# Two weight conversions dealt out in steps over the last attention blocks, and the first v's split queued behind the centroid copies

## The chip, the cores and the metric

The kernel runs on one core of a Trainium2 chip. The metric is device time in microseconds (us), the median over runs; less is better. TensorE is PE, its weight load PEld, VectorE DVE, ScalarE ACT, GpSimd POOL; SyncE (SP) issues every DMA of this kernel.

## The reference, cut to what matters

Three parts follow each other: clustered attention, a product of two projections (moe), and a gated one (moe2).

```python
mask = q_assign[:, :, :, None] == k_assign[:, :, None, :]   # argmax over 16 centroids per head
scores = scale * q @ k.T; scores = where(mask, scores, -1e9)
x = softmax(scores) @ v                                     # 2 x 8 heads, 768 tokens, head size 64
x = x.transpose(0, 2, 1, 3).reshape(1536, 512)
h = ((x @ w1) * (x @ w2)) @ w3                              # 512 -> 1024 -> 1024
y = h @ w_out                                               # 1024 -> 512
out = (sigmoid(y @ w_gate) * (y @ w_val)) @ w_out2          # 512 -> 1536 -> 512
```

The weights reach the chip as 64-bit floats (two 32-bit words each) and are converted there. Every operand of a large product is split into a high and a low part (`hi`, `lo`), and a product is three matmuls (L65 to L67).

## The kernel before, in words

**Attention.** The 16 heads make 8 pairs (`pr`), each pair has two heads (`e`), each head three blocks of 256 queries: 48 blocks (`NB`), block number = 6 pr + 3 e + q0/256. The main loop runs `i` from -2 to 48. In one turn it issues the scores 2i+3 and 2i+4 (two 128-query halves of blocks i+1 and i+2: matmuls L315 to L318, then the maximum `nm` on DVE, L319, and the exponential `e` on ACT, L321), the transposes of block i (PE L332, `ph` on ACT L56, `pl` on DVE L59), and the weighted sum with v of block i-1 (L355, L356). So a block has two `nm`, and the scores of turn i = 33 end with the first half of block 35.

**Preparation of a pair** runs beside the blocks of the pair before it: loads of q and k (`load_qk`, L192) and v; splits into hi and lo (`prep_split`: q's on ACT and DVE, k's on POOL for pairs above 0); similarities with the centroids (`prep_sims`, PE L252); the cluster by argmax and its one-hot code (L254 to L277); and DMAs inside SBUF that build the operands QH, KH, QX, KX (`move`, L62).

**The start.** Before pair 0 the centroids are normalised, transposed by PE (L164) and split into `chi` and `clo` on DVE (L168, L169). Eight small POOL copies put them into `cw` (L175), which `prep_sims` needs as weights. `prep_v(0)` splits v on POOL (two L54, two L59). PE runs `warm` transposes (L134) whose result nobody reads: 12, 8, and 70 after the first similarities.

**Conversion of weights** (`f64_split`): a DMA brings a 128x512 tile of 64-bit words (L98, pool tag f64 with 3 buffers), ACT takes the absolute value of the upper words (L102), DVE does five operations in a row (L108 clamp, L110 shift, L111 merge, L112 mask, L113 product; "steps" here), `f_engine` adds (L114), ACT rounds to hi (L115), POOL subtracts for lo (L116). `load_pair` does this twice, for w1 and w2 of one group. The first two pairs of w1 and w2 are converted within attention, at i = NB-12 = 36 and i = NB-6 = 42, each as a whole, with L114 on POOL:

```python
if i in (NB - 12, NB - 6):
    with tc.issue_after(last["DVE"].ins), tc.issue_after(last["ACT"].ins):
        wt.append(load_pair(w12, len(wt), "w12_", nc.gpsimd))
```

`tc.issue_after(x)` puts every instruction of the block that runs on x's engine behind x in that engine's queue. It is a lower bound on the place only. Otherwise each engine's order is set by a list scheduler from the order of the text, its own estimate of when operands are ready, and buffers; an instruction that is ready by that estimate can go ahead of earlier text. Within a queue the order is then fixed, and a waiting instruction holds up all behind it.

**After attention** (L400 on) everything is a long run of matmuls `p` (L65 to L67): first `g_unit`, which needs the two converted pairs, then the other products.

Of the kernel before, what the change touches and what calls it, by code (L numbers as in the profile page):

```python
# [9 lines left out]
F32R = mybir.dt.float32r  # L10
U32 = mybir.dt.uint32
# [5 lines left out]
NP = H // 2  # L17
# [10 lines left out]
def tile_cluster_attention__then__moe__then__gated_moe(  # L28
# [15 lines left out]
    nc = tc.nc  # L44
# [6 lines left out]
    def split(x, hi, lo, hi_engine, lo_engine):  # L51

        if hi_engine is nc.gpsimd:
            nc.gpsimd.tensor_scalar(out=hi, in0=x, scalar1=1.0, scalar2=1.0, op0=ALU.mult, op1=ALU.mult)  # L54
        elif hi_engine is nc.scalar:
            nc.scalar.copy(hi, x)  # L56
        else:
            nc.vector.tensor_copy(hi, x)
        lo_engine.tensor_tensor(out=lo, in0=x, in1=hi, op=ALU.subtract)  # L59
# [20 lines left out]
    ws = ctx.enter_context(tc.tile_pool(name="ws", bufs=2, side="right"))  # L80
# [3 lines left out]
    def f64_split(src, hi, lo, name, f_engine, lo_engine):  # L84

        n = src.shape[-1]
        raw = ws.tile([128, n, 2], U32, tag="f64", name=f"{name}_f64", bufs=3)
        nc.sync.dma_start(raw.rearrange("p n t -> p (n t)"), src.bitcast(U32))  # L98
        low, high = raw[:, :, 0], raw[:, :, 1]
        a = ws.tile([128, n], U32, tag="f64a", name=f"{name}_a", bufs=3)  # L100
        af = a.bitcast(F32)
        nc.scalar.activation(af, high.bitcast(F32), AF.Abs)  # L102
        if cvp:
            nc.gpsimd.tensor_scalar(out=af, in0=af, scalar1=F64_MAX, scalar2=F64_MIN, op0=ALU.min, op1=ALU.max)
            t = cvp["pool"].tile([128, n], U32, tag="t", name=f"{name}_t", bufs=2)
            tf = t.bitcast(F32)
        else:
            nc.vector.tensor_scalar(out=af, in0=af, scalar1=F64_MAX, scalar2=F64_MIN, op0=ALU.min, op1=ALU.max)  # L108
            t, tf = a, af
        nc.vector.tensor_scalar(out=t, in0=a, scalar1=3, scalar2=0x3FFFFFF8, op0=ALU.logical_shift_left, op1=ALU.bitwise_and)  # L110
        nc.vector.scalar_tensor_tensor(out=high, in0=high, scalar=0xC0000000, in1=t, op0=ALU.bitwise_and, op1=ALU.bitwise_or)  # L111
        nc.vector.tensor_scalar(out=t, in0=high, scalar1=0xFF800000, scalar2=None, op0=ALU.bitwise_and)  # L112
        nc.vector.scalar_tensor_tensor(out=tf, in0=low, scalar=2.0 ** -52, in1=tf, op0=ALU.mult, op1=ALU.mult)  # L113
        f_engine.tensor_tensor(out=af, in0=high.bitcast(F32), in1=tf, op=ALU.add)  # L114
        nc.scalar.copy(hi, af)  # L115
        lo_engine.tensor_tensor(out=lo, in0=af, in1=hi, op=ALU.subtract)  # L116

    def load_pair(src, m, what, f_engine=None):
        hl = ws.tile([128, 2, 2, NP, 128], F32R, tag="hl", name=f"{what}{m}")
        for w in range(2):  # L120
            f64_split(src[m, w], hl[:, 0, w].rearrange("p k c -> p (k c)"), hl[:, 1, w].rearrange("p k c -> p (k c)"),
                      f"{what}{m}_{w}", f_engine or nc.vector, nc.gpsimd)
        return hl

    att, cst = ExitStack(), ExitStack()
# [44 lines left out]
    for e in range(2):  # L170
        rows = slice(64 * e, 64 * e + 64)
        for w in range(2):
            base = 64 * w + 32 * e
            for g, src in ((0, chi), (1, clo)):
                nc.gpsimd.tensor_copy(  # L175
                    cw[rows, :, w, base + 16 * g : base + 16 * g + 16],
                    src[rows].bitcast(F32).rearrange("p (n e c) -> p n e c", n=NP, e=2)[:, :, e, :],
                )
# [5 lines left out]
    core = att.enter_context(tc.tile_pool(name="core", bufs=2))  # L184


    raw = {}

    def load_qk(pr):
        for w in range(2):  # L190
            t = core.tile([128, S], F32, tag="raw", name=f"raw{pr}_{w}", bufs=2)
            nc.sync.dma_start(t, qkT[pr, :, w, :])  # L192
            raw[pr, w] = t

    def load_v(pr):
        t = core.tile([128, 2, KT, D], F32, tag="vraw", name=f"vraw{pr}", bufs=1)
        nc.sync.dma_start(t, v[pr])
        raw[pr, "v"] = t


    load_qk(0)


# [24 lines left out]
    def prep_scatter(pr, e):  # L228
        qh, ql, kh, kl = opnd[pr, "hl"]
        r = slice(64 * e, 64 * e + 64)  # L230
        QH = core.tile([96, S], F32R, tag="QH", name=f"QH{pr}_{e}", bufs=3)
        KH = core.tile([96, S], F32R, tag="KH", name=f"KH{pr}_{e}", bufs=3)
        QX = core.tile([128, S], F32R, tag="QX", name=f"QX{pr}_{e}", bufs=3)
        KX = core.tile([128, S], F32R, tag="KX", name=f"KX{pr}_{e}", bufs=3)
        move(QH[0:64], qh[r])
        move(KH[0:64], kh[r])
        move(QX[0:64], qh[r])
        move(QX[64:128], ql[r])
        move(KX[0:64], kl[r])
        move(KX[64:128], kh[r])  # L240
        opnd[pr, e] = (QH, KH, QX, KX)
# [17 lines left out]
    def prep_argmax(pr):  # L259
        sm = opnd.pop((pr, "sm"))  # L260
        mx = core.tile([128, S // 32], F32, tag="mx", name=f"mx{pr}", bufs=2)
        shape = [128, S // 32, C]
        nc.vector.tensor_reduce(out=mx, in_=sm, axis=AX.X, op=ALU.max)
        nc.vector.tensor_tensor(out=sm, in0=sm, in1=mx.unsqueeze(2).broadcast_to(shape), op=ALU.is_ge)
        lead(pr).tensor_tensor(out=sm, in0=sm, in1=dec.unsqueeze(1).broadcast_to(shape), op=ALU.mult)
        opnd[pr, "code"] = sm
# [13 lines left out]
    def prep_mask(pr, e):  # L280
        ohT = opnd[pr, "oh"]
        QH, KH, _, _ = opnd[pr, e]
        if pr == 0:
            nc.scalar.copy(QH[64:96], ohT[32 * e : 32 * e + 32])
            nc.vector.tensor_scalar(out=KH[64:96], in0=ohT[64 + 32 * e : 96 + 32 * e], scalar1=-1.0, scalar2=BIG, op0=ALU.add, op1=ALU.mult)
            return
        move(QH[64:96], ohT[32 * e : 32 * e + 32])
        move(KH[64:96], ohT[64 + 32 * e : 96 + 32 * e])

    def prep_v(pr):  # L290
        vr = raw.pop((pr, "v"))
        for e in range(2):
            vx = core.tile([128, KT, 2, D], F32R, tag="vx", name=f"vx{pr}_{e}", bufs=3)
            split(vr[:, e], vx[:, :, e, :], vx[:, :, 1 - e, :], nc.gpsimd, nc.gpsimd)
            opnd[pr, e, "v"] = vx
# [1 line left out]

    blocks = [(pr, e, q0) for pr in range(NPR) for e in range(2) for q0 in range(0, S, 256)]
    NB = len(blocks)
    exps, pts, avs, acc_x, last = {}, {}, {}, {}, {}  # L300

    def scores(j):

# [84 lines left out]
    def finish_x(pr):  # L388
        b, hp = divmod(pr, NP)
        xa, r = acc_x.pop((pr, "xa")), acc_x.pop((pr, "r"))  # L390
        nc.gpsimd.tensor_tensor(out=xa, in0=xa, in1=r, op=ALU.mult)
        split(xa, x_hl[:, hp, 0, S * b : S * b + S], x_hl[:, hp, 1, S * b : S * b + S], nc.gpsimd, nc.gpsimd)
# [10 lines left out]
    prep_onehot(0)  # L403
    for e in range(2):
        prep_mask(0, e)
    prep_v(0)
    load_qk(1)
    prep_split(1)
    prep_scatter(1, 0)
    wt = []  # L410
    for i in range(-2, NB + 1):
        pr, at = divmod(i, 6)
        nxt = pr + 1 if 0 <= i and pr + 1 < NPR else None
        later = nxt + 1 if nxt and nxt + 1 < NPR else None
        scores(2 * i + 3)
        if nxt and at == 1:
            prep_scatter(nxt, 1)
            prep_argmax(nxt)
        transposes(i, 0)
        if nxt and at == 0:  # L420
            prep_sims(nxt)
        scores(2 * i + 4)
        if nxt and at == 2:
            prep_onehot(nxt)
            for e in range(2):
                prep_mask(nxt, e)
        transposes(i, 1)
        transposes(i, 2)
        if later and at == 2:
            load_qk(later)  # L430
        if later and at == 3:
            load_v(later)
        if i == 0:
            load_v(1)
        weighted_v(i - 1, 0)
        if nxt and at == 2:
            prep_v(nxt)
        weighted_v(i - 1, 1)
        if 0 < pr and i < NB and at == 2:
            finish_x(pr - 1)  # L440
        weighted_v(i - 1, 2)
        if later and at == 3:
            prep_split(later)
            prep_scatter(later, 0)
        if 0 <= i < NB and at == 5:
            sums(pr)
        if i in (NB - 12, NB - 6):
            with tc.issue_after(last["DVE"].ins), tc.issue_after(last["ACT"].ins):
                wt.append(load_pair(w12, len(wt), "w12_", nc.gpsimd))
    finish_x(NPR - 1)  # L450
    att.close()

# [81 lines left out]
    for u, tok in enumerate(units):  # L534
        for c in range(NP):
            p = ps.tile([128, 512], F32, tag="p", name=f"p3_{c}_{u}")
# [14 lines left out]
    for g in range(MG // GS):  # L551
        us = []
        wo2 = p5.tile([128, GS, 2, DM], F32R, tag="wo2", name=f"wo2_{g}", bufs=2)
        for j in range(GS):
            m = g * GS + j
# [11 lines left out]
        for t in range(T // 128):  # L567
            p = ps.tile([128, DM], F32, tag="p", name=f"p5_{g}_{t}")
# [67 lines left out]
```

## Time and profile before

| | |
|---|---|
| median of 3 runs | 816.96 us (816.45 to 820.29) |
| profiled execution | 818.45 us, its span 816.6 us |
| mean granted clock of TensorE in the span | 0.985 of full |
| busy share of the span | PE 95%, DVE 71%, ACT 44%, POOL 42% |
| DMA | 78.05 MB, mean 96 GB/s |
| last `nm` of attention begins | 270.07 us |
| first matmul `p` of the products begins | 277.25 us |

A timeline row gives the start in us, the time in us, engine, line, operation, what is written and read, the tile, how many instructions were merged into the row, and in brackets the idle time of the engine before it with what ended it. A time with "x2" is that of both, from the start of the first to the end of the last.

### The profile page before, as it was taken

The page shows a single profiled execution, that of the slowest core. Times are in us where ns is not written, and L with a number is a line of the kernel's source. Part 1 is how long each engine was busy: PE and PEld are TensorE (multiplying, and loading weights), DVE is VectorE, ACT ScalarE, POOL GpSimd, SP SyncE. Part 2 cuts the span into 40 slices and gives each one's busy share as a digit, 9 for nine tenths or more (in the row PEclk, how much of TensorE's full clock was granted, in tenths as well). Part 3 has the DMA queues.
Part 4 walks back from the last instruction along what each step waited for, and adds up shares of the span by engine and source line. Part 5 has one row for each costly group of instructions (what it writes and reads, how often), then busy time and mean ns, then how long its engine had stood idle before and what let it go on. Part 6 is the DMA issues. An engine that isn't in the chain of part 4 may idle for free.

```text
span 816.6 us, 11246 instructions
## 1 busy us (share of the span) xinstructions
PE 777.5 (95%) x4051; PEld 662.7 (81%) x4051; DVE 580.5 (71%) x856; ACT 360.8 (44%) x711; POOL 342.4 (42%) x356
## 2 busy tenths in 40 slices
PE   6899999999696999999999999999999999999998
PEld 6788888988595888887888888888888888888886
DVE  3898989989978769999999443377761777827222
ACT  1788889889586633344433222223231322012100
POOL 3347657757646354545443111234420444124100
PEclk8999999999888999999999999999999999999999
DMA  8745646556512033444442200022220122200012
GB/s 220 212 132 136 169 124 172 144 132 165 137 42 72 21 130 106 151 130 142 142 155 78 77 1 1 26 77 79 78 80 24 52 77 96 86 1 0 1 65 90
DMA packets 26967, 78.05 MB, mean 96 GB/s; under 512 B 4416, under 2 KB 4512, under 8 KB 26912
## 3 DMA queue, kind: packets, MB, share of 16 engines
q1 hardware_dynamic: 26912, 77.33, 32.2%
q8 instruction: 32, 0.52, 0.3%
q14 instruction: 23, 0.19, 0.1%
HBM read 52.49 MB, written 3.19 MB: 68 GB/s over the span
## 4 chain that ended last, share of the span: by engine, by line
PE 67%; DVE 12%; POOL 8%; ACT 5%; DMA 4%; issue 4%; SPq 0%; DVEq 0%; POOLq 0%; ACTq 0%
PE p L66 17%; PE p L67 17%; PE p L65 17%; PE pt L332 3%; DVE nm L319 2%; DMA raw<-in_qkT_dram 2%; ACT e L321 2%; PE s L315 1%; DVE pl L59 1%; PE sims L252 1%; PE av L356 1%; PE w34p L67 1%; PE av L355 1%; PE w34p L65 1%; PE w34p L66 1%
## 5 line engine op out<-in xcount | busy, mean ns | idle before, releaser
L65 PE MATMUL p<-x,wgv 128*128 128x512 f32 x288 | 112.0, 389 | 0.0
L66 PE MATMUL p<-x,wgv 128*128 128x512 f32 x288 | 112.0, 389 | 0.0
L67 PE MATMUL p<-x,wgv 128*128 128x512 f32 x288 | 112.0, 389 | 0.0
L319 DVE TENSOR_REDUCE nm<-s 128x1 f32<-128x768 f32 x96 | 90.9, 948 | 10.4 <-PE s L318 9.8
L332 PE MATMUL pt<-ident,e 128*128 128x128 f32 x576 | 83.6, 279 | 10.4 <-DVE pl L59 9.5
L59 DVE TENSOR_TENSOR pl<-pt,ph 128x512 fp32r<-128x512 f32 x128 | 85.3, 682 | 7.7 <-ACT ph L56 6.8
L321 ACT ACTIVATE e<-s,nm 128x768 f32<-128x768 f32 x96 | 87.4, 910 | 3.7 <-DVE nm L319 2.8
L332 PEld LDWEIGHTS pt<-ident,e 128*128 128x128 f32 x576 | 68.6, 144 | 15.3 <-DVE pl L59 9.9
L56 ACT CAST ph<-pt 128x512 fp32r<-128x512 f32 x128 | 72.8, 588 | 17.7 <-PE pt L332 11.1
L355 PE MATMUL av<-ph,vx 128*128 128x256 f32 x288 | 77.4, 301 | 1.6 <-ACT xb L367 1.6
L356 PE MATMUL av<-pl,vx 128*128 128x256 f32 x288 | 75.4, 294 | 2.0 <-POOL pl L59 1.8
L65 PE MATMUL p<-x,w 128*128 128x512 f32 x192 | 74.8, 390 | 0.0
L66 PE MATMUL p<-x,w 128*128 128x512 f32 x192 | 74.7, 389 | 0.0
L67 PE MATMUL p<-x,w 128*128 128x512 f32 x192 | 74.7, 389 | 0.0
L54 POOL TENSOR_SCALAR u<-ut 128x512 fp32r<-128x512 f32 x36 | 22.4, 622 | 112.1 <-DVE ut L562 112.1
L65 PEld LDWEIGHTS p<-x,wgv 128*128 128x128 f32 x288 | 54.1, 188 | 11.3
L67 PEld LDWEIGHTS p<-x,wgv 128*128 128x128 f32 x288 | 54.1, 188 | 11.2
L66 PEld LDWEIGHTS p<-x,wgv 128*128 128x128 f32 x288 | 54.1, 188 | 11.1
L116 POOL TENSOR_TENSOR wo<-wo_a,wo 128x512 fp32r<-128x512 f32 x20 | 26.3, 1316 | 80.6 <-ACT wo L115 80.6
L59 DVE TENSOR_TENSOR u<-ut,u 128x512 fp32r<-128x512 f32 x36 | 35.7, 991 | 34.2 <-POOL u L54 32.9
L356 PEld LDWEIGHTS av<-pl,vx 128*128 128x128 f32 x288 | 56.5, 196 | 3.2 <-POOL pl L59 3.0
L355 PEld LDWEIGHTS av<-ph,vx 128*128 128x128 f32 x288 | 56.0, 194 | 2.9 <-ACT xb L367 2.2
(146 smaller groups left out, 1850.6 us busy)
## 6 DMA issues: line engine op xcount, KB each, us to landing
wgv_f<-in_w_gv_dram SPq DMA_DIRECT2D x24, 512.0 KB, 3.2
wo_f<-in_w_out_dram SPq DMA_DIRECT2D x20, 512.0 KB, 3.4
w_f<-in_w_dram SPq DMA_DIRECT2D x16, 512.0 KB, 3.3
w_f<-in_w3T_dram SPq DMA_DIRECT2D x16, 512.0 KB, 3.2
raw<-in_qkT_dram SPq DMA_DIRECT2D x16, 384.0 KB, 4.5
vraw<-in_v_dram SPq DMA_DIRECT2D x8, 384.0 KB, 3.9
QH<-hi SPq DMA_DIRECT2D x16, 192.0 KB, 2.5
KH<-hi SPq DMA_DIRECT2D x16, 192.0 KB, 2.9
```

What stands on the lines that cost most here:

```text
L54: nc.gpsimd.tensor_scalar(out=hi, in0=x, scalar1=1.0, scalar2=1.0, op0=ALU.mult, op1=ALU.mult)
L56: nc.scalar.copy(hi, x)
L59: lo_engine.tensor_tensor(out=lo, in0=x, in1=hi, op=ALU.subtract)
L65: nc.tensor.matmul(ps, whi, xhi, start=start, stop=False)
L66: nc.tensor.matmul(ps, whi, xlo, start=False, stop=False)
L67: nc.tensor.matmul(ps, wlo, xhi, start=False, stop=stop)
L116: lo_engine.tensor_tensor(out=lo, in0=af, in1=hi, op=ALU.subtract)
L319: last["DVE"] = nc.vector.tensor_reduce(out=nm, in_=sp[:, 0:S], axis=AX.X, op=ALU.max, negate=True)
L321: last["ACT"] = nc.scalar.activation(et, sp[:, 0:S], AF.Exp, bias=nm, accum_out=ss[:, at : at + 1])
L332: nc.tensor.transpose(pt[:, kk, 128 * t : 128 * t + 128], es[t][:, k0 : k0 + 128], ident)
L355: nc.tensor.matmul(av, w, ph[:, kk, :], start=kt == 0, stop=False)
L356: nc.tensor.matmul(av, w, pl[:, kk, :], start=False, stop=kt == KT - 1)
```

## The change

`f64_split` is divided into a load (`f64_load`) and a generator (`f64_steps`) that pauses after each of its five DVE operations. The two whole conversions at i = 36 and 42 go. From i = 33 to 47, `convert` is called twice per turn, behind the turn's last `nm` and `e`: each call lets one DVE operation out; the call after a tile's fifth puts out the tile's L114 (POOL), L115 (ACT) and L116 (POOL), and goes on with the next tile's L102 (ACT) and first DVE operation. Four tiles need 21 calls, so the last one falls into the turn i = 43. Three of the four tiles are loaded at i = 28, behind the last DMA of `load_qk`, the fourth at i = 38. `prep_v(0)` is put behind the last of the eight centroid copies in POOL's queue.

```diff
+    def f64_load(src, name):
+        raw = ws.tile([128, src.shape[-1], 2], U32, tag="f64", name=f"{name}_f64", bufs=3)
         nc.sync.dma_start(raw.rearrange("p n t -> p (n t)"), src.bitcast(U32))
+        return raw
+
+    def f64_steps(raw, hi, lo, name, f_engine, lo_engine):
...
             nc.vector.tensor_scalar(out=af, in0=af, scalar1=F64_MAX, scalar2=F64_MIN, op0=ALU.min, op1=ALU.max)
+            yield
             t, tf = a, af
         nc.vector.tensor_scalar(out=t, in0=a, scalar1=3, scalar2=0x3FFFFFF8, op0=ALU.logical_shift_left, op1=ALU.bitwise_and)
+        yield
         nc.vector.scalar_tensor_tensor(out=high, in0=high, scalar=0xC0000000, in1=t, op0=ALU.bitwise_and, op1=ALU.bitwise_or)
+        yield
         nc.vector.tensor_scalar(out=t, in0=high, scalar1=0xFF800000, scalar2=None, op0=ALU.bitwise_and)
+        yield
         nc.vector.scalar_tensor_tensor(out=tf, in0=low, scalar=2.0 ** -52, in1=tf, op0=ALU.mult, op1=ALU.mult)
+        yield
...
-                nc.gpsimd.tensor_copy(
+                cw_done = nc.gpsimd.tensor_copy(
...
-            nc.sync.dma_start(t, qkT[pr, :, w, :])
+            last["SP"] = nc.sync.dma_start(t, qkT[pr, :, w, :])
...
-    prep_v(0)
+    with tc.issue_after(cw_done.ins):
+        prep_v(0)
...
+    def convert():
+        while first or steps:
+            if not steps:
+                m, w = first.pop(0)
+                hi, lo = (wt[m][:, p, w].rearrange("p k c -> p (k c)") for p in range(2))
+                steps.append(f64_steps(raws.pop(0), hi, lo, f"w12_{m}_{w}", nc.gpsimd, nc.gpsimd))
+            if next(steps[0], True) is None:
+                return
+            steps.pop(0)
...
-        if i in (NB - 12, NB - 6):
-            with tc.issue_after(last["DVE"].ins), tc.issue_after(last["ACT"].ins):
-                wt.append(load_pair(w12, len(wt), "w12_", nc.gpsimd))
+        if i == NB - 20:
+            with tc.issue_after(last["SP"].ins):
+                raws = [f64_load(w12[m, w], f"w12_{m}_{w}") for m, w in first[:3]]
+        if i == NB - 10:
+            raws.append(f64_load(w12[1, 1], "w12_1_1"))
+        if NB - 15 <= i < NB:
+            for _ in range(2):
+                with tc.issue_after(last["DVE"].ins), tc.issue_after(last["ACT"].ins):
+                    convert()
```

## Rows read from the trace of the kernel before

**Rows 1.** Windows by stretch: each engine's busy us, PEclk, DMA share, GB/s.

```profile
300.00:400.00 100.00, 99.67 (x440) 82.17 (x440) 90.09 (x146) 41.65 (x71) 49.25 (x52) 1.00 0.40 132
```

**Rows 2.** Timeline of PE at the start.

```profile
12.11 1.22 PE L252 MATMUL sims<-hi,cw 128*128 128x512 f32 x2 [4.68 <-POOL cw L175]
...
16.12 7.71 PE L134 MATMUL warm<-ident 128*128 128x128 f32 x62
23.58 0.48 PE L315 MATMUL s<-KH,QH 96*128 96x512 f32 x1
...
30.21 0.72 PE L252 MATMUL sims<-hi,cw 128*128 128x512 f32 x2
```

**Rows 3.** Timeline of POOL at the start.

```profile
7.61 0.99 POOL L54 TENSOR_SCALAR vx<-vraw 128x384 fp32r<-128x384 f32 x2 [4.63 <-DMA vraw<-in_v_dram]
...
11.37 0.87 POOL L175 CAST cw<-clo 64x64 fp32r<-64x64 f32 x4
```

**Rows 4.** Timeline of DVE at the start.

```profile
5.66 0.29 DVE L169 TENSOR_TENSOR clo<-cps,chi 128x128 fp32r<-128x128 f32 x1
...
6.74 0.95 DVE L59 TENSOR_TENSOR lo<-raw,hi 128x768 fp32r<-128x768 f32 x1
16.36 0.98 DVE L254 STREAM_TRANSPOSE sT<-sims 128x768 f32<-128x768 f32 x1 [8.67 <-PE sims L252]
...
22.07 1.34 DVE L285 TENSOR_SCALAR KH<-ohT 32x768 fp32r<-32x768 f32 x2
```

**Rows 5.** Timeline of DVE: first nm of blocks 32, 38 and 47.

```profile
179.21 0.95 DVE L319 TENSOR_REDUCE nm<-s 128x1 f32<-128x768 f32 x1
...
208.24 0.95 DVE L319 TENSOR_REDUCE nm<-s 128x1 f32<-128x768 f32 x1
...
267.65 0.95 DVE L319 TENSOR_REDUCE nm<-s 128x1 f32<-128x768 f32 x1
```

**Rows 6.** Windows: an undisturbed block, and the stretch before block 38.

```profile
240.80:244.81 4.01, 4.01 (x33) 3.75 (x32) 3.63 (x6) 3.95 (x10) 0.00 (x0) 1.00 0.00 0
201.21:208.24 7.03, 6.46 (x47) 5.54 (x45) 5.39 (x8) 5.11 (x12) 3.32 (x3) 1.00 0.51 116
```

**Rows 7.** Timeline of DVE in the two conversions.

```profile
211.73 3.07 DVE L108 TENSOR_SCALAR w_a<-w_a 128x512 f32<-128x512 f32 x2
...
253.20 2.29 DVE L111 SCALAR_TENSOR_TENSOR w_f<-w_f,w_a 128x512 uint32<-128x512 uint32 x1
255.42 0.41 DVE L110 TENSOR_SCALAR w_a<-w_a 128x512 uint32<-128x512 uint32 x1
...
256.09 0.68 DVE L111 SCALAR_TENSOR_TENSOR w_f<-w_f,w_a 128x512 uint32<-128x512 uint32 x1
```

**Rows 8.** Timeline of POOL beside the second conversion.

```profile
253.08 1.86 POOL L59 TENSOR_TENSOR x<-xa,x 128x768 fp32r<-128x768 f32 x1
```

**Rows 9.** Windows for the conversions' tile w_a alone: busy us of DVE, ACT, POOL.

```profile
208.00:261.00 53.00, 17.98 (x20) 4.39 (x7) 8.00 (x6) 0.86 0.27 72
```

**Rows 10.** Line L273: durations ns min/median/max, first and last start.

```profile
L273 DVE TENSOR_TENSOR oh<-sm,mc x8: 547/708/1574, 20.5 to 228.4; 128x384 f32<-128x384 f32 x8
```

**Rows 11.** Waits between 208 and 278 us: total, times, longest.

```profile
ACT w L115 <- POOL w_a L114: 13.9, 4, 6.1
```

**Rows 12.** Timeline of POOL: the k of pair 6 arrives.

```profile
173.68 0.83 POOL L54 TENSOR_SCALAR hi<-raw 128x768 fp32r<-128x768 f32 x1 [2.95 <-DMA raw<-in_qkT_dram]
```

**Rows 13.** Timeline of SP at the start: q of pair 1 is issued.

```profile
17.96 0.33 SPq L192 DMA_DIRECT2D raw<-in_qkT_dram  x1
```

**Rows 14.** Windows: clock beside PE's busy share.

```profile
167.72:171.58 3.86, 3.06 (x24) 2.65 (x22) 3.83 (x7) 3.80 (x9) 1.89 (x2) 1.00 0.96 266
...
210.00:220.00 10.00, 4.74 (x35) 4.09 (x33) 9.93 (x13) 5.16 (x13) 6.80 (x6) 0.95 0.66 157
220.00:230.00 10.00, 8.25 (x36) 7.62 (x37) 7.10 (x12) 6.05 (x13) 9.55 (x8) 0.53 0.33 105
```

**Rows 15.** Chain of waits: four transposes within the slow stretch.

```profile
226.43 0.85 PE pt L332 x4
```

More of the change, by code (lines that the diff above doesn't have):

```diff
@@ L84, in f64_split @@
     def f64_split(src, hi, lo, name, f_engine, lo_engine):
-        n = src.shape[-1]
-        raw = ws.tile([128, n, 2], U32, tag="f64", name=f"{name}_f64", bufs=3)
+        for _ in f64_steps(f64_load(src, name), hi, lo, name, f_engine, lo_engine):
+            pass
+    def f64_load(src, name):
+        raw = ws.tile([128, src.shape[-1], 2], U32, tag="f64", name=f"{name}_f64", bufs=3)
         nc.sync.dma_start(raw.rearrange("p n t -> p (n t)"), src.bitcast(U32))
+        return raw
+    def f64_steps(raw, hi, lo, name, f_engine, lo_engine):
+        n = raw.shape[1]
         low, high = raw[:, :, 0], raw[:, :, 1]
@@ L116, in f64_split, with load_pair @@
         lo_engine.tensor_tensor(out=lo, in0=af, in1=hi, op=ALU.subtract)
-    def load_pair(src, m, what, f_engine=None):
+    def load_pair(src, m, what):
         hl = ws.tile([128, 2, 2, NP, 128], F32R, tag="hl", name=f"{what}{m}")
         for w in range(2):
-            f64_split(src[m, w], hl[:, 0, w].rearrange("p k c -> p (k c)"), hl[:, 1, w].rearrange("p k c -> p (k c)"),
-                      f"{what}{m}_{w}", f_engine or nc.vector, nc.gpsimd)
+            hi, lo = (hl[:, p, w].rearrange("p k c -> p (k c)") for p in range(2))
+            f64_split(src[m, w], hi, lo, f"{what}{m}_{w}", nc.vector, nc.gpsimd)
         return hl
@@ L184, in tile_cluster_attention__then__moe__then__gated_moe @@
     core = att.enter_context(tc.tile_pool(name="core", bufs=2))
-    raw = {}
+    raw, last = {}, {}
     def load_qk(pr):
@@ L299, in tile_cluster_attention__then__moe__then__gated_moe @@
     NB = len(blocks)
-    exps, pts, avs, acc_x, last = {}, {}, {}, {}, {}
+    exps, pts, avs, acc_x = {}, {}, {}, {}
     def scores(j):
@@ L409, in tile_cluster_attention__then__moe__then__gated_moe @@
     prep_scatter(1, 0)
-    wt = []
+    wt = [ws.tile([128, 2, 2, NP, 128], F32R, tag="hl", name=f"w12_{m}") for m in range(2)]
+    first, steps = [(m, w) for m in range(2) for w in range(2)], []
+    def convert():
[7 more added lines that the diff above has]
+            steps.pop(0)
     for i in range(-2, NB + 1):
```

## The prediction, made blind

> **What bounds the kernel now.** I read the windows by stretch first. After attention PE is busy 99.67 of 100 us at full clock while DVE, ACT and POOL have room [rows 1]; nothing that the change touches lies there, so from the first `p` matmul to the end the time is taken as fixed, and a gain must come from attention, which ends at about 277 us. In attention there are two places that the change touches.
>
> At the start, the timeline of PE shows 4.68 us without work ahead of the similarities, ended by the centroid copies on POOL [rows 2]. The timeline of POOL says why the copies are late: v's split stands ahead of them and itself waits for v's DMA until 7.61, so the last copies only run from 11.37 to 12.24 [rows 3], while `clo`, their last input, is there at 5.95 [rows 4].
>
> In the last blocks, the starts of the maxima on DVE give the pace [rows 5]. From block 32 to 38, six blocks with all preparation take 29.03 us. In this the last block takes 7.03 us, because PE's similarities of the next pair wait there; an undisturbed block without them takes 4.01 us and PE is busy through all of it [rows 6]. So six blocks after block 38, which have no similarities to wait for, would take 29.03 - (7.03 - 4.01) = 26.0, and three more 12.0. From block 38 to 47 it would be 38.0; the trace has 59.4. The two whole conversions, each a burst on DVE's queue that holds up the maxima and `pl` behind it, therefore cost 21.4 us.
>
> **The start, step by step.** With v's split behind them the copies start when `chi` is there and `clo` at 5.95 lets the second four go; four take 0.87 [rows 3, 4], so they end at about 7.4 at the latest if the first four begin at 5.65. The similarities also need the low part of k, which DVE finishes at 7.69 [rows 4]; only part of the eight matmuls does. I start them at 7.5 instead of 12.11. At full clock two take 0.72 [rows 2], and eight (half of them half as long) at most 2.2; I take 1.8: end at 9.3 instead of about 16.1. The chain of DVE from the first transpose to the operand KH is 16.36 to 22.07 plus half of 1.34 [rows 4], 6.4 us, and would end at about 16. But 70 `warm` transposes stand ahead of the first scores in PE's queue, 62 of which took 7.71 [rows 2]; 68 or so after the similarities take 8.4 and end at 17.4 to 17.7. So the warm-ups, not the clusters, end last: first scores at about 17.4 instead of 23.58. **Gain 6.2.** The most is 7.2 (if a few warm-ups fall into the wait before); the least 2.5, from the other thing that pair 1 waits for, below.
>
> What is late next: v's split moves from 7.61 to about 7.4 to 7.6, as v arrives only then; POOL has nothing else to do until q of pair 1, and the first weighted sum comes later still, so this costs nothing. In SP's queue the three early weight loads (1.5 MB) no longer share the DMAs of the start, a help for which I count nothing.
>
> **The last blocks: what is put back.** The burst goes, so 21.4 come off; twenty DVE steps, four ACT absolute values and casts, and eight POOL operations return, spread over the turns i = 33 to 43. The price of a DVE step is open. Without disturbance a one-input step takes 0.41 and a two-input one 0.68 [rows 7]; three and two of them per tile, four tiles: 10.4 us. The same kinds also took 1.54 each (L108) and 2.29 (L111) [rows 7], and the second lasted until just after POOL's 1.86 us subtraction had ended [rows 8]; all steps like that would be 4 x (3 x 1.54 + 2 x 2.29) = 36.8. Together the twenty took 17.98 [rows 9]. A single DVE operation between two SBUF operands that stands alone among the blocks, like the new steps, is L273: 0.55 at best, 0.71 in the median, 1.57 once [rows 10]. It is the nearest row: about 0.2 more than clean, 4 for twenty, so I take **14.4**.
>
> Not all of this lengthens a block. DVE idles 1.64 of the 7.03 us before block 38 and 0.38 in an undisturbed block of the last pair [rows 6]; over the eleven blocks I let 3 of it be used. Of the ACT and POOL work I count only the standstill of ACT ahead of the cast, which waits for POOL's sum: 13.9 us in four such waits now [rows 11], all within the bursts. Spread out the sum is hardly late, and I put back 1.5 (from 0 to 6). Put back in all: 14.4 - 3 + 1.5 = 12.9. **Gain 8.5.** Best: clean steps, 5 absorbed, no waits, 21.4 - 5.4 = 16. Worst: 21.4 - 36.8 - 6, a loss of 21.
>
> **The moved loads.** Three of 0.5 MB go out at i = 28, right behind the load of k of pair 6. POOL's split of that k ends a wait for its DMA at 173.68 [rows 12], and the similarities of pair 6 wait for the split. FIFO order would cost nothing; if the 1.5 MB shared the way with k evenly, k (0.4 MB) could be some 4 us late, by the 266 GB/s of that stretch [rows 14]. **Loss 1**, between 0 and 4. The operands of pair 6, queued behind, have until block 36; the fourth load finds an empty queue.
>
> **Sum.** -6.2 - 8.5 + 1.0 = -13.7. The profiled execution's own time of 818.45 becomes 804.75; it was 1.49 above the median of 816.96, from which I get **803.3**.
>
> **Rivals.**
>
> *Port (17%).* The twenty steps stay as dear as they are, 18.0, because POOL, with its sums and subtractions of `pl`, x and v, is busy for two thirds of the stretch, and each step waits for what runs there [rows 7 to 9, 14]. Against it: the median of L273. Put back 18 - 3 + 1.5 = 16.5, gain 4.9, sum -10.1: 806.9. The Trainium skill, "SBUF — State Buffer", section "Who interferes with whom", says that a VectorE operation with two SBUF inputs, or in a mode with two ports, and a GpSimd operation exclude each other for their whole length. The L111 that outlasts POOL's subtraction agrees with that rule; the short median of L273 says only that it seldom comes to it.
>
> *Clean steps (13%).* Nearly all is hidden or undisturbed: gain 16 in the last blocks, 7 at the start, no DMA price: 794. For it: PE is busy for 4.01 of a 4.01 us block, and DVE has its slack beside it; against it: with preparation DVE has next to none.
>
> *The start gives less (10%).* Pair 1 depends on SP, which issues q of pair 1 at 17.96 [rows 13], and on the DMAs ahead of it in that queue; if those don't move up, only 2.5 of the 6.2 remain: 807.
>
> *Nothing spreads (5%).* The text's edges say only "not before". If the steps slide together or behind, a burst with 21.4 stays, and only the start is gained: 811.
>
> *Slower, by the clock (4%).* The mechanism: every block gets a small wait of PE, and TensorE falls to its lower level for the whole of the last blocks. Full clock was granted where PE was busy 79% of a stretch (3.06 of 3.86); after a stretch with 47% it fell, and the next shows 0.53, near its lower level of 1.2 GHz [rows 14]. My blocks have PE busy 4.0 of some 5.2 us, 77%: close to the first. At the lower level four transposes took 0.85, 0.21 each, against 0.12 for a warm one [rows 15, 2]; a block of 4.0 would take 8.0, 2.8 more than my 5.2. The point from which this decides is 13.7 / 2.8, about five blocks; with all eleven it is +31: 834. The Trainium skill, "TensorE: Matmul & The Clock Gate", section "A second HAM failure mode: psum-queue depth-cycling", tells of a kernel whose short, frequent idle times made the clock swing; no row here shows that with waits as short as these.
>
> **How the numbers follow.** My forecast has the remaining 51%; predicted 803.3. Its own bounds (start 5 to 7, last blocks 4 to 13, loads 0 to 3) reach from about 797 to 810. Port and the poor start lie within that. Clean steps lie just below it and are taken in to 794; "nothing spreads" at 811 is taken in; the clock case is left out. Range 794 to 812. A measurement of this kernel can tell about 0.5% (4 us) from no change: faster means below 812.9. Faster: forecast, port, clean, start, and half of "nothing spreads", less 2 for mishaps: 0.91. Same 0.05, slower 0.04.
>
> **What would show it.** In the changed profile: copies before v's split on POOL, similarities at 7.5, first `nm` near 18.4 instead of 24.57; no stretch in the last blocks with PE below 70% and no fall of the clock there; blocks 35 to 45 of 5 to 5.5 us; the twenty steps at 14 to 15 us in all; block 47 at 267.65 - 13.7 = 254, the first `p` near 263.5, and everything behind as long as before. I'm wrong if first `nm` stays above 22, if the steps cost over 18, if k of pair 6 arrives over 2 us later against its neighbours, or if the time after the first `p` changes by over 1 us.

## The result, and the profile after

The changed kernel takes 808.12 us (median of 4 runs, 807.62 to 808.46) beside 816.71 for the kernel before on the same chip: ratio 0.9887, 95% interval 0.9856 to 0.9917, faster by 1.1%. It lies within the range of 794 to 812, 4.8 us above the 803.3 that was predicted. Its profiled execution took 808.15 us, with a span of 806.3.

Where the time came from, by the start of the maxima `nm` on DVE in the two profiles:

| start of | before | after | difference |
|---|---|---|---|
| first nm (block 0) | 24.57 | 20.27 | -4.30 |
| first nm of block 5 | 47.22 | 46.27 | -0.95 |
| first nm of block 32 | 179.21 | 177.48 | -1.73 |
| first nm of block 47 | 267.65 | 257.52 | -10.13 |
| end of the span | 816.64 | 806.30 | -10.34 |

The first nm of block 0 and of block 5, before and after:

```profile
24.57 1.82 DVE L319 TENSOR_REDUCE nm<-s 128x1 f32<-128x768 f32 x2 [1.16 <-PE s L318]
...
47.22 0.94 DVE L319 TENSOR_REDUCE nm<-s 128x1 f32<-128x768 f32 x1
```

```profile
20.27 1.82 DVE L332 TENSOR_REDUCE nm<-s 128x1 f32<-128x768 f32 x2 [0.75 <-PE s L331]
...
46.27 0.94 DVE L332 TENSOR_REDUCE nm<-s 128x1 f32<-128x768 f32 x1
```

So the rest after block 47 is as long as before (549.0 and 548.8), blocks 32 to 47 gave 8.4 us (forecast with the loads: 7.5), and of 4.3 us won at the start (forecast 6.2) only about 1 was left five blocks later. A profile is one execution. The one of the kernel before was 1.7 us above its median, and the same last blocks, not edited, took 85.6 us instead of 88.4 in the profile of experiment 1, so one profile against one leaves the 8.4 open by some 3 us.

**The start.** Timeline of PE in the changed kernel:

```profile
8.81 1.22 PE L265 MATMUL sims<-hi,cw 128*128 128x512 f32 x2 [2.42 <-POOL cw L188]
...
12.47 6.93 PE L147 MATMUL warm<-ident 128*128 128x128 f32 x62
19.27 0.50 PE L328 MATMUL s<-KH,QH 96*128 96x512 f32 x1
...
25.00 0.50 PE L328 MATMUL s<-KH,QH 96*128 96x512 f32 x1 [4.06 <-ACT e L334]
```

These answer to [rows 2]: the similarities start 3.3 us earlier instead of 4.6, the first scores at 19.27 instead of 17.4; and then a new wait of 4.06 us, for the first exponential. POOL and DVE show why the similarities weren't earlier:

```profile
5.77 1.63 POOL L188 CAST cw<-chi 64x64 fp32r<-64x64 f32 x4 [2.79 <-DVE chi L181]
7.45 1.50 POOL L188 CAST cw<-clo 64x64 fp32r<-64x64 f32 x4
9.03 0.98 POOL L54 TENSOR_SCALAR vx<-vraw 128x384 fp32r<-128x384 f32 x2
```

```profile
5.89 0.96 DVE L231 SCALAR_TENSOR_TENSOR lo<-raw,hi 128x768 fp32r<-128x768 f32 x1
7.17 1.04 DVE L59 TENSOR_TENSOR lo<-raw,hi 128x768 fp32r<-128x768 f32 x1 [0.32 <-ACT hi L56]
```

Four copies take 1.63 and 1.50 us, where four took 0.87 [rows 3]: they now run beside DVE's two subtractions, which read two operands from SBUF. Only two of the eight are slow, one beside each subtraction; the other six take 0.23 to 0.24 us as before:

```profile
5.95 0.99 POOL L188 CAST cw<-chi 64x64 fp32r<-64x64 f32 x1
...
7.45 0.86 POOL L188 CAST cw<-clo 64x64 fp32r<-64x64 f32 x1
```

They end at 6.94 and 8.31, each 0.1 us after its subtraction (6.85 and 8.21). The windows view shows the second loss, PE at the lower clock (0.50, which is 1.2 GHz) while the similarities run (PE, PEld, DVE, ACT, POOL, then PEclk); the first row is the changed kernel, the second the similarities of the kernel before:

```profile
8.60:12.00 3.40, 3.19 (x11) 2.61 (x12) 0.00 (x0) 0.00 (x0) 3.28 (x6) 0.50 0.97 230
```

```profile
12.10:16.10 4.00, 3.99 (x14) 3.41 (x15) 0.00 (x0) 0.00 (x0) 0.14 (x1) 0.50 1.03 240
```

This fall is not the same in every execution: in the profiles of experiments 3, 4, 5, 6, 7, 10 and 12 the clock stays full here, and the first nm starts at 18.80 to 18.94; in those of 1, 8, 9 and 11 it falls too, and the first nm starts at 20.26 to 20.43.

The timeline of ACT has what took most of the gain back:

```profile
21.81 0.83 ACT L56 CAST hi<-raw 128x768 fp32r<-128x768 f32 x1 [1.74 <-POOL raw L235]
22.66 1.28 ACT L334 ACT_TABLE_LOAD   x1
23.95 0.90 ACT L334 ACTIVATE e<-s,nm 128x768 f32<-128x768 f32 x1
```

The cast of pair 1's q (`hi<-raw`) now stands ahead of the first exponential and waits for POOL's scaling of that q, which waits for its data; the load of the exponential's table and the exponential itself, whose maximum is there at about 21.2, queue behind it. Before the change the exponential came first:

```profile
25.56 0.90 ACT L321 ACTIVATE e<-s,nm 128x768 f32<-128x768 f32 x1 [0.49 <-DVE nm L319]
...
26.45 0.82 ACT L56 CAST hi<-raw 128x768 fp32r<-128x768 f32 x1
```

Behind its wait of 4.06 us PE also works at the lower clock for 3.4 us:

```profile
25.70:29.10 3.40, 3.40 (x16) 3.21 (x15) 1.92 (x2) 1.73 (x6) 1.03 (x1) 0.50 0.87 195
```

In the profiles of experiments 1, 3, 8, 9, 11 and 12, where the exponential comes first, the clock doesn't fall there.

**The last blocks.** First nm of blocks 35 and 36 in the kernel before, then of blocks 32, 35, 36 and 47 in the changed kernel, answering to [rows 5]:

```profile
191.84 0.93 DVE L319 TENSOR_REDUCE nm<-s 128x1 f32<-128x768 f32 x1
...
197.35 0.95 DVE L319 TENSOR_REDUCE nm<-s 128x1 f32<-128x768 f32 x1
```

```profile
177.48 0.95 DVE L332 TENSOR_REDUCE nm<-s 128x1 f32<-128x768 f32 x1
...
189.83 0.94 DVE L332 TENSOR_REDUCE nm<-s 128x1 f32<-128x768 f32 x1
...
197.96 0.95 DVE L332 TENSOR_REDUCE nm<-s 128x1 f32<-128x768 f32 x1
...
257.52 0.96 DVE L332 TENSOR_REDUCE nm<-s 128x1 f32<-128x768 f32 x1 [0.41 <-PE s L331]
```

Blocks 32 to 47 take 80.04 us for 88.44. Of this stretch PE was busy for 72.79 us before and 70.14 now, at a mean clock of 0.90 and 0.98 (windows; PE first, PEclk third from the end; before, then after):

```profile
179.21:267.65 88.44, 72.79 (x490) 66.10 (x488) 77.89 (x106) 66.92 (x146) 55.98 (x48) 0.90 0.38 101
```

```profile
177.48:257.52 80.04, 70.14 (x486) 62.55 (x485) 74.80 (x106) 66.49 (x145) 55.19 (x48) 0.98 0.48 131
```

So of the 8.4 us, 5.75 are idle time of PE and 2.65 busy time; the clock was low for 17.1 us of this stretch before and for 3.4 now. The bursts are gone, but the step to block 36, before most of the conversion steps, takes 8.13 us; before it took 5.51. The twenty DVE steps together, from the windows of tile `w_a` (DVE, ACT, POOL), cost 16.47 us for 17.98 [rows 9]:

```profile
190.00:255.00 65.00, 16.47 (x20) 5.72 (x9) 9.99 (x8) 0.97 0.44 120
```

The issues on SP, before and after, and POOL's timeline tell of block 36:

```profile
177.65 0.50 SPq L381 DMA_DIRECT2D r_dram<-rt  x1
...
181.40 1.19 SPq L385 DMA_DIRECT2D r<-r_dram  x2
```

```profile
175.87 1.77 SPq L101 DMA_DIRECT2D w_f<-in_w_dram  x3
177.75 0.34 SPq L394 DMA_DIRECT2D r_dram<-rt  x1
...
185.96 1.11 SPq L398 DMA_DIRECT2D r<-r_dram  x2
```

```profile
190.93 1.83 POOL L404 TENSOR_TENSOR xa<-xa,r 128x768 f32<-128x768 f32 x1 [2.10 <-DVE nm L332]
192.85 0.83 POOL L290 TENSOR_SCALAR ohT<-ohT 64x768 f32<-64x768 f32 x1
```

The three weight loads (1.5 MB) stand just ahead of the row sums' small write (`r_dram`). The read back `r`, which needs that write landed, is issued at 185.96, 8.2 us behind it; in the kernel before, 3.75 us behind (177.65 to 181.40). POOL's product with `r` (L404) waits, and behind it in POOL's queue stands the mask of pair 6, which block 36 needs by one more DMA. That this path is what lengthens the block is argued, not shown: the row puts the wait down to DVE's `nm`, which ends at 190.8, and PE stands idle for only 0.89 of the 8.13 us (7.24 busy with 57 matmuls; 5.37 of 5.51 with 41 before). Much of the longer step is other work that PE's queue now has ahead of the scores of block 36. That it comes with the moved loads is shown by experiments 9 to 12.

### The profile page after: what moved, and what is told of

Same layout as the page of the kernel before. It is cut to its first block, busy times and chain, and to the rows that moved or that the text cites. A ratio compares the mean times of both kernels' runs of the same rounds, so it can differ in the third digit from the quotient of the medians.

```text
span 806.3 us, 11235 instructions
## 1 busy us (share of the span) xinstructions
PE 775.2 (96%) x4051; PEld 660.6 (82%) x4051; DVE 578.7 (72%) x856; ACT 360.4 (45%) x711; POOL 342.7 (43%) x356
## 4 chain that ended last, share of the span: by engine, by line
PE 69%; DVE 11%; POOL 6%; ACT 5%; DMA 4%; issue 3%; SPq 1%; DVEq 0%; POOLq 0%; ACTq 0%
PE p L67 18%; PE p L66 18%; PE p L65 18%; PE pt L345 3%; DVE nm L332 2%; PE s L328 2%; ACT e L334 2%; PE av L369 2%; DVE pl L59 1%; PE av L368 1%; PE s L330 1%; PE w34p L67 1%; ACT ph L56 1%; PE w34p L65 1%; PE sims L265 1%
## 5 line engine op out<-in xcount | busy, mean ns | idle before, releaser
L345 PE MATMUL pt<-ident,e 128*128 128x128 f32 x576 | 85.6, 281 | 2.8 <-DVE pl L59 2.6
L369 PE MATMUL av<-pl,vx 128*128 128x256 f32 x288 | 73.7, 288 | 5.5 <-POOL pl L59 5.2
L596 DVE TENSOR_TENSOR ut<-p,ut 128x512 f32<-128x512 f32 x36 | 24.7, 686 | 44.4 <-PE p L67 44.3
```

The costliest lines, as they stand in the source:

```text
L345: nc.tensor.transpose(pt[:, kk, 128 * t : 128 * t + 128], es[t][:, k0 : k0 + 128], ident)
L369: nc.tensor.matmul(av, w, pl[:, kk, :], start=False, stop=kt == KT - 1)
L596: nc.vector.tensor_tensor(out=ut, in0=pv, in1=ut, op=ALU.mult)
```

## The experiments

A ratio is to the runs of the kernel before on the same chip; the changed kernel has 0.9887 (0.9856 to 0.9917). Experiments 1 to 4, 5 to 8 and 9 to 12 ran on one chip each, so run times are compared within such a group and ratios across them.

**1. The split of v alone** (weights as before):

```diff
...
-    prep_v(0)
+    with tc.issue_after(cw_done.ins):
+        prep_v(0)
```

> The v split behind the centroid copies alone, weights as before. In the changed kernel the first maximum came 4.3 us earlier (20.27 for 24.57), but block 2 only 0.96 us earlier (31.92 for 32.88). Theory A (queue order on ACT): the changed kernel put the cast of pair 1's q ahead of the first exponential in ACT's queue; here the exponential stands first, as before, so block 2 should come 2.5 to 4 us earlier than 32.88 and the time should be 2.5 to 4 us below before (813 to 814.5). Theory B (pair 1 sets it): the data of pair 1 and its similarities set block 2 whatever ACT does; block 2 near 32 and the time about 1 us below before (815.8).

Measured: 813.65, ratio 0.9954 (0.9934 to 0.9974); block 5 at 43.65, 3.57 us earlier than before, though the first nm (20.36) is no earlier than in the changed kernel. ACT's timeline of this kernel:

```profile
19.87 1.28 ACT L321 ACT_TABLE_LOAD   x1
21.36 0.90 ACT L321 ACTIVATE e<-s,nm 128x768 f32<-128x768 f32 x1 [0.20 <-DVE nm L319]
...
22.30 0.83 ACT L56 CAST hi<-raw 128x768 fp32r<-128x768 f32 x1
```

The exponential is first again and starts 2.6 us earlier than in the changed kernel, as theory A said. This kernel also has its weight loads at the start, so experiment 3 is the direct test.

**2. The steps and the moved loads alone.**

```diff
-    with tc.issue_after(cw_done.ins):
-        prep_v(0)
+    prep_v(0)
```

> The steps and the moved loads alone, v's split ahead of the copies as before. If the gain of the changed kernel is that of the last blocks (block 32 to 47 in 80.0 us for 88.4), then about 8 us below before (808 to 809.5), near the changed kernel. If the two parts need each other, clearly less than 7 us.

Measured: 808.84, ratio 0.9894 (0.9860 to 0.9929). Blocks 32 to 47 in 78.6 us; block 36 again takes 8.46. The two parts alone would sum to -1.5%; together they gave -1.1%: 0.9894 and 0.9887 are not apart by more than the noise, so the v part gives next to nothing on top of the other.

**3. The first exponential first.** `prep_split(1)` is traced behind the first scores:

```diff
-    prep_split(1)
-    prep_scatter(1, 0)
...
         scores(2 * i + 4)
+        if i == -2:
+            with tc.issue_after(last["ACT"].ins):
+                prep_split(1)
+            prep_scatter(1, 0)
```

> The changed kernel with pair 1's q cast put behind the first exponential on ACT. Theory A: the first exponential begins near 21.5 instead of 23.95, block 2 comes 2 to 3 us earlier than 31.92, and the time is 2 to 3 us below the changed kernel (805 to 806). Theory B: the exponential is earlier, but block 2 and the time stay (808 plus or minus 0.7).

Measured: 805.71, ratio 0.9856 (0.9821 to 0.9892), in which the gain over the changed kernel is not clear of noise. In the trace the exponential starts at 19.91 and block 5 at 42.53 (46.27 in the changed kernel). Of these 3.7 us, 1.5 were there at the first nm (18.80), where the clock didn't fall in this execution. But an early first nm alone is worth little: experiments 4, 5, 7 and 10 have it at 18.89 to 18.94 with the cast still ahead, and reach block 5 at 45.7 to 45.9 (experiment 6 at 47.4). So 3.2 us or more of the 3.7 come from the queue. At block 47 only 1.9 are left (255.59); the step to block 36 takes 10.06 here.

**4. Without the DVE steps.** The five DVE operations of each of the four tiles are left out; the first one:

```diff
-            nc.vector.tensor_scalar(out=af, in0=af, scalar1=F64_MAX, scalar2=F64_MIN, op0=ALU.min, op1=ALU.max)
```

> The changed kernel without the twenty DVE steps (the weights of the first two groups are left unconverted); loads, ACT and POOL operations stay. Blocks 32 to 47 took 80.0 us; undisturbed by the sum 67.0. If DVE's time sets what is put back (14.4 of steps less 3 of idle, 1.5 for ACT and POOL): 68 to 70 us, time 10 to 12 us below the changed kernel (796 to 798). Rival: a good part comes from ACT's and POOL's added operations and the waits between the engines: 73 to 76 us, 802 to 804.

**5. Without POOL's operations**, steps kept:

```diff
+        if name.startswith("w12_") and not cvp:
+            nc.scalar.copy(hi, tf)
+            nc.scalar.copy(lo, tf)
+            return
         f_engine.tensor_tensor(out=af, in0=high.bitcast(F32), in1=tf, op=ALU.add)
```

> The changed kernel with its twenty DVE steps, but without POOL's eight operations of the two conversions (the sum of the two words is left out, and a second cast on ACT stands in for the low part). Without the steps but with POOL's operations, blocks 32 to 47 took 76.0 us, against 80.0 with both and 67.0 for undisturbed blocks by the sum. Theory (POOL's queue): most of the rest is POOL's, whose queue also holds the pl of every third transposes and the one-hot mask; here 71 to 76 us, the time 4 to 8 us below the changed kernel. Rival (DVE's steps): 78 to 80 us, the time within 2 us of it.

**6. Without either.** Both edits, the casts reading `af`:

```diff
+        if bare:
+            nc.scalar.copy(hi, af)
+            nc.scalar.copy(lo, af)
+            return
```

> The changed kernel without the twenty DVE steps and without POOL's eight operations; ACT writes both parts (12 operations in the blocks). This measures the undisturbed blocks themselves: by the sum 67.0 us from block 32 to 47, up to 69 with ACT's work, the time near 796. If it is above 71, the 67.0 was wrong, and what was counted as put back by the conversions was there anyway.

Measured: 802.6 (0.9824, 0.9792 to 0.9856), 805.6 (0.9860, 0.9831 to 0.9888) and 802.92 (0.9825, 0.9798 to 0.9853). First nm of block 32 and of block 47, in the three kernels:

```profile
175.28 0.94 DVE L336 TENSOR_REDUCE nm<-s 128x1 f32<-128x768 f32 x1
...
251.33 0.95 DVE L336 TENSOR_REDUCE nm<-s 128x1 f32<-128x768 f32 x1
```

```profile
174.88 0.95 DVE L336 TENSOR_REDUCE nm<-s 128x1 f32<-128x768 f32 x1
...
253.42 0.95 DVE L336 TENSOR_REDUCE nm<-s 128x1 f32<-128x768 f32 x1
```

```profile
178.03 0.95 DVE L340 TENSOR_REDUCE nm<-s 128x1 f32<-128x768 f32 x1
...
252.07 0.95 DVE L340 TENSOR_REDUCE nm<-s 128x1 f32<-128x768 f32 x1
```

That is 76.05, 78.54 and 74.04 us; the changed kernel has 80.04. Experiments 4 and 5 came out near what their rivals said. With neither, the blocks take 74.0, not 67.0: by that run's own expectation, 7 us of what was called put back were there anyway. On this floor DVE's steps add 4.5, POOL's operations 2.0, both 6.0; leaving operations out can also change the order of the queues, so these are prices in this program. In time the kernel without either is no faster than the one without steps, because its first blocks came out longer: block 32 starts at 178.03 instead of 175.28. The floor could not have been 67.0: without either, PE is busy for 69.94 of these 74.04 us at full clock, and in no profile for less than 69.0.

```profile
178.03:252.07 74.04, 69.94 (x495) 61.66 (x494) 60.42 (x86) 68.20 (x149) 44.65 (x40) 1.00 0.51 142
```

One thing that holds the floor up besides is the mask. In the run without steps PE waits for it in the step to block 42, which takes 8.2 us:

```profile
228.15 0.47 PE L332 MATMUL s<-KH,QH 96*128 96x512 f32 x1 [1.92 <-DMA KH<-ohT]
```

**7. Four turns later.**

```diff
-        if i == NB - 10:
+        if i == NB - 6:
...
-        if NB - 15 <= i < NB:
+        if NB - 11 <= i < NB:
```

> The changed kernel with the steps four turns later (i = 37 to 47; the fourth load at i = 42), where pair 7 has no preparation and POOL was idle most of the time. If the put back comes from the company (POOL's queue and DVE full of preparation): blocks 32 to 47 in 75 to 78 us, the time 2 to 5 us below the changed kernel. Rival: the same work costs the same wherever it is, or comes late for the first products: within 1 us of it, or above.

Measured: 809.89, ratio 0.9933 (0.9891 to 0.9974); blocks 32 to 47 in 80.8. A miss: the emptier last pair didn't help. The steps to blocks 41 and 46 took 8.3 and 7.5; why was not tested. The rest after block 47 takes 551.7 us instead of 548.8, so the rival's other half, that the work comes late for the first products, agrees with the trace.

**8. The sum on DVE**, in `convert`, on the kernel of experiment 3:

```diff
-                steps.append(f64_steps(raws.pop(0), hi, lo, f"w12_{m}_{w}", nc.gpsimd, nc.gpsimd))
+                steps.append(f64_steps(raws.pop(0), hi, lo, f"w12_{m}_{w}", nc.vector, nc.gpsimd))
```

> The kernel with the first exponential ahead on ACT, and the sum of the two words (L114 of before) on DVE instead of POOL in the two conversions. POOL's queue theory: 5 us less on POOL, 2.5 us more on DVE: blocks 32 to 47 shorter by 1 to 3 us than the 80.3 of the kernel with the first exponential ahead. DVE theory: longer by 1 to 3.

Measured: 807.96, ratio 0.9890 (0.9855 to 0.9925); blocks 32 to 47 in 83.4, 3.0 longer than in experiment 3. Four more operations of 0.7 us on DVE cost about their own time, although 5 us left POOL: the DVE theory in sign. Its size is not shown. PE's idle time in these blocks grew by only 1.1 us (10.0 to 11.0); the other 2.0 are PE's busy time (70.4 to 72.3), with the lower clock twice in this profile and once in that of experiment 3.

**9. The loads early again.** One edge of the change is undone, so the three loads go back to the start:

```diff
-            with tc.issue_after(last["SP"].ins):
+            if True:
                 raws = [f64_load(w12[m, w], f"w12_{m}_{w}") for m, w in first[:3]]
```

> The changed kernel with one thing undone: the three loads have no edge, so they stand at the start again, as before the change. Theory: the moved loads cost twice: at the start, where without them the order of ACT's queue came out with pair 1's cast ahead of the first exponential (here the exponential is first again: block 5 near 43.6 instead of 46.3), and before block 36, where the 1.5 MB stood ahead of the row sums' small DMA (r_dram), so that the block took 8.1 us for 5.5 (here 5.5 to 6). Together 4 to 6 us below the changed kernel: 802 to 804. Rival: the loads at the start delay pair 1 by as much, within 1 us of the changed kernel.

Measured: 803.96 (801.79 to 805.06), ratio 0.9828 (0.9805 to 0.9851), below the changed kernel's interval and the best of all that convert the weights. Block 5 starts at 43.32. SP's row sums and the nm of blocks 35 and 36:

```profile
172.49 0.50 SPq L394 DMA_DIRECT2D r_dram<-rt  x1
...
176.22 1.19 SPq L398 DMA_DIRECT2D r<-r_dram  x2
```

```profile
186.81 0.94 DVE L332 TENSOR_REDUCE nm<-s 128x1 f32<-128x768 f32 x1
...
192.02 0.95 DVE L332 TENSOR_REDUCE nm<-s 128x1 f32<-128x768 f32 x1
```

The read follows the write after 3.7 us, and block 36 takes 5.21. Both costs of the moved loads are gone, as expected. Of the 2.9 us that block 36 is shorter than in the changed kernel, 1.7 come back in block 37 (5.74 instead of 4.08). Block 38 is 1.2 shorter, but in it the changed kernel had its 3.4 us at the lower clock. Of the three loads only one is issued before the first scores (at 3.06, as before the change); the other two follow at 19.96.

**10. The loads one by one**, each behind the reads of `r`, which set `last["SP"]` here. **11.** The same with the edit of experiment 3. **12.** As 11, with the mask's scaling on DVE. The cores of 10 and 12:

```diff
-        if i == NB - 20:
+        if i in (NB - 18, NB - 15, NB - 12, NB - 9):
+            m, w = divmod(len(loaded), 2)
             with tc.issue_after(last["SP"].ins):
-                raws = [f64_load(w12[m, w], f"w12_{m}_{w}") for m, w in first[:3]]
-        if i == NB - 10:
-            raws.append(f64_load(w12[1, 1], "w12_1_1"))
+                raws.append(f64_load(w12[m, w], f"w12_{m}_{w}"))
+            loaded.append(0)
```

```diff
-            nc.gpsimd.tensor_scalar(out=ohT[64:128], in0=ohT[64:128], scalar1=-1.0, scalar2=BIG, op0=ALU.add, op1=ALU.mult)
+            nc.vector.tensor_scalar(out=ohT[64:128], in0=ohT[64:128], scalar1=-1.0, scalar2=BIG, op0=ALU.add, op1=ALU.mult)
```

> The changed kernel with the four loads one at a time (i = 30, 33, 36, 39), the first behind the reads of the row sums of pair 4. The start is as in the changed kernel. Theory: block 36 takes 5.5 to 6 us for 8.1, the time 2 to 3 us below the changed kernel (805.5 to 806.5). Rival: block 36 waits for something else (POOL's queue ahead of the mask) and stays above 7.5, the time within 1 us.

> The loads one at a time and the first exponential ahead on ACT. If the two are independent: block 5 near 42.5, block 36 at 5.5 to 6 us, 4.5 to 6 us below the changed kernel: 802 to 804. If something else takes up the slack: above 805.

> As the one before, and the scaling of the one-hot mask of pairs 1 to 7 (L290 of the changed kernel) on DVE instead of POOL. Theory: the first scores of each pair wait for the chain one-hot, POOL's queue, DMA; with POOL's queue out of it the longer blocks of each pair shorten by 0.5 to 1.5 us: 3 to 8 us below the one before (795 to 800). Rival: DVE is full there, and the 0.5 us each come back: within 1.5 us of it.

Measured: 806.86 (0.9867, 0.9846 to 0.9888), 805.54 (0.9849, 0.9826 to 0.9871) and 808.96 (0.9895, 0.9876 to 0.9914). In all three block 36 takes 5.0 to 5.3, so it was the loads. But experiment 10 gave only 0.2% (1.6 us), within the noise and less than expected: the step to block 41 took 7.6 for 5.9. And 11 was not the sum of its parts: blocks 32 to 47 in 79.4, hardly below the 80.3 of experiment 3; 76.9 where the loads were early. Loads in the last blocks seem to cost in more places than one; which, is open. In 12 the mask on DVE, seven operations of 0.71 us on average, cost 3.4 us over 11: little of their 5.0 us found idle time on DVE. Neither expectation, faster by 3 to 8 or within 1.5, came true.

## Why the prediction was right, and where its steps were wrong

**Sign, size and cause in the main: right.** Faster, from the last blocks, by the burst that went (experiment 2 has nearly the whole gain without the v part); the rest after attention unchanged. The range held, and none of the four signs of being wrong appeared: the first nm is at 20.27, the steps cost 16.5, pair 6's k came early, and from the first `p` to the end it takes 540.2 us instead of 539.4.

**The start, 6.2: wrong.** The step that failed is the sentence "So the warm-ups, not the clusters, end last: first scores at about 17.4", and with it the silent assumption that an earlier first score stays earlier. The warm-ups did end last, about level with the first operand: they end at 19.40, `QH` on ACT at 19.22. But the similarities ahead of them started 1.3 us late, because of the copies beside DVE, and took 3.8 us instead of 1.8. The sum had taken full clock for them, although in the kernel before they ran at 0.50; at full clock they took 2.3 (experiment 3). The 62 warm-ups behind them took 6.93 instead of 7.71, which had been timed partly at the lower clock. The sum's own 9.3 and 8.4 also make 17.7, not the 17.4 that was taken.

The first scores came 4.3 us earlier, and so did the first nm. Of these 4.3, 3.4 were lost in five blocks; with the exponential first, experiment 1 lost 0.6. So most of the loss is ACT's queue, with the clock that fell behind PE's wait. The early weight loads, for whose absence "I count nothing", were what mattered: with them at the start the exponential came out first (experiments 1 and 9), without them the cast did (2, and the changed kernel). The rival "the start gives less" had the right size, 2.5 or less. It named pair 1's q, and the cast did wait for that; but the delay came by ACT's queue, which the rival didn't have.

**The moved loads, 1: undersized, and at another place.** The price was sought at pair 6's k, which was not late: its split starts at 171.97 instead of 173.68, as much earlier as block 32. It was paid behind the row sums' write: 2.6 us at block 36 against the kernel before; against experiments 9 to 11, 1.3 to 2.1 over blocks 36 and 37 together. It was within its bounds of 0 to 4.

**The last blocks, 8.5: right by luck, two errors that cancel.** Undisturbed blocks were put at 67.0 from the fastest neighbours; they take 74.0 with neither steps nor POOL's part in them, 2.6 of the difference being block 36. PE's busy time alone, 69 us and more, rules the 67.0 out. Put back were not 12.9 but 6.0. The steps cost 16.5 in DVE time, not 14.4, nearer to the port rival's 18.0; without POOL's eight operations they took 17.1, so it was not the conversions' own POOL work that held them up. But the 16.5 lengthened the blocks by 4.0 to 4.5 only. A likely reason, seen at one block in experiment 4 and not tested, is that in long blocks something else is late anyway, such as the mask.

**The clock rival: did not happen.** The clock in the last blocks fell once, for 3.4 us at 203, instead of 17.1 in the two bursts.

## What to carry to other kernels

When a load is moved in a program whose queues a list scheduler fills, look again at the order of every queue that its absence touches: here moving three DMAs reordered ACT, and took back most of another edit's gain. Ask of each transfer what small, dependent transfer stands behind it in the same queue. And don't take the fastest neighbouring block as the undisturbed one: set the sum beside the busy time of the engine that limits it, or leave the work out and measure the floor.

## What the runs showed of the hardware that was not expected

Four POOL copies of 64x64 took 0.87 us alone [rows 3] and 1.50 to 1.63 beside DVE subtractions with two SBUF operands. In each four it is one copy that is held, until 0.1 us after the subtraction's end; the other three keep their 0.23 to 0.24. The Trainium skill, "SBUF — State Buffer", section "Who interferes with whom", says that such a pair exclude each other; the rows agree, and show that it is not only DVE that waits: here short POOL operations ahead of the similarities paid. In the other direction the rule is not enough to price a step: the same twenty steps took 16.5 us spread out and 18.0 in bursts, while the clean price is 10.4.
